# Ten wide idle products at the head of a retention and MLP kernel become 42 narrow ones

## The chip, the cores and the metric

The kernel runs on one core of a Trainium2 chip. A core has a matrix engine (TensorE, PE in the profile; its weight loads are listed apart as PEld), three engines for elementwise work (VectorE = DVE, ScalarE = ACT, GpSimd = POOL), a fifth that only issues transfers (SyncE = SP), and 16 DMA engines. Each engine works off its own stream of instructions in order, and the engines wait for each other by semaphores. The metric is the device time of one execution in microseconds (us); lower is better.

## The reference

Two stages follow each other. The first is a retention: attention without softmax, with a decay per head. For 8 batches, 8 heads, 576 positions and head dimension 64:

```python
scores = scale * np.matmul(q, k.transpose(0, 1, 3, 2))
Dmat = np.where(rel >= 0, gamma[:, None, None] ** rel, 0.0)   # rel = query position - key position
attn = np.matmul(scores * Dmat, v)
```

Its output, turned to 4608 tokens by 512 features, goes through a feed-forward layer with a "snake" activation and 2048 hidden features:

```python
h = x @ w_in
s = np.sin(alpha * h)
out = (h + s * s / (alpha + 1e-9)) @ w_out
```

All inputs and the output are in float32.

## The kernel before

The products are made in float16 and summed in float32. The decay is separable, so q and k are multiplied by powers of gamma when they are cast (`cast`, L126, by a table `cn`), and only a triangular mask is left for the scores. The 512 first positions of a batch are worked as two parts p of 256 positions, each in two chunks of 128; what earlier chunks contribute comes through a running state of 64 x 64 per head. The 64 last positions of all batches are worked at the end (`Ends`).

For one batch, the steps on TensorE are: `turn` (L189) transposes q and k by products with an identity; `scores` (L325) makes k times q in quadrants of 64 x 64; `outer` (L262) makes the sums of k times v for the state; `values` (L353) multiplies the masked scores with v, once for `same` False and once for True, and TensorE drains between the two (`change_rows`, L214); `add_states` (L385) adds what the state contributes. `masked` (L342, VectorE) applies the mask, `take_sum`, `more`, `next_sum` and `to_state` make the states (ScalarE, GpSimd, VectorE), and `keep` (L403) casts the result to xT, the input of the second stage. In this stage a product is small: 64 or 128 columns, so many instructions pass in a short time.

The second stage works on 512 tokens at a time (n = 0 to 8). `project(n, fc)` (L501) makes 128 of the 2048 hidden features with four products of 512 columns; `sine` (ScalarE), `square` (one of three engines) and `product` (VectorE) make the activation gT; `gemm2(n, u)` (L547) adds four products of 512 columns to an output tile, and `finish` writes it. The weights are loaded once, by GpSimd's queue, in four groups each: `load_w_in(g)` (L91) and `load_w_out(g)` (L95), 512 KB a group in float16.

The order of everything is written out by hand. Under `tc.manual_schedule()` (L582) the order of the calls is the order of each engine's stream. The first blocks are interleaved call by call (L583 to L1067): attention of batch 0, then `project` of block 0 mixed with attention of batch 1, and so on. From block 3 on a loop (L1072) places the attention of batch n + 1, mostly at unit 12 of the 16 units of block n, between the second stage's steps.

At the head TensorE has nothing to do until q and k have arrived and been cast. There `keep_busy` (L562) puts idle products on it: products of a tile of zeros with itself, whose result nobody reads. Each product has its own weight load ahead of it, so one idle product is two instructions. A call takes a PSUM tile under a tag, and the first product of a call waits for the last product of the call before it with the same tag. There are four calls ahead of the first `turn` (L593 to L596), of 2, 8, 10 and 4 products of 512 columns; the first waits for the tile of zeros (L591) alone. Two further calls, of 4 products and 1, stand among the steps of batch 0 (L616, L636).

Behind the head, in TensorE's order: `turn` of q and k, part 0; `turn` of k, part 1; scores(0, 1); idle products; `turn` of q, part 1; outer, scores, outer and two more scores; one idle product; values(0, False); a small transpose of alpha; values(0, True); add_states(0); values(1, False), values(1, True), add_states(1); project(0, 0) in two halves, for which the first group of w_in must be there; and project(0, 6) (L664), the first product that needs the second group.

The lines that the change touches, and the function:

Of the kernel before, what the change touches and what calls it, by code (L numbers as in the profile page):

```python
# [17 lines left out]
def kernel(  # L18
# [543 lines left out]
    def keep_busy(n, tag, m=512):  # L562
        idle = psum.tile([P, 512], F32, tag=tag, bufs=1, name="idle")
        for _ in range(n):
            matmul(idle[:, 0:m], zero[:, 0:P], zero[:, 0:m], start=True, stop=True)
# [16 lines left out]
    with tc.manual_schedule():  # L582
# [9 lines left out]

        keep_busy(2, "h0")  # L593
        keep_busy(8, "op")
        keep_busy(10, "op")
        keep_busy(4, "op")  # L596
        load(0, "q", 0)
        cast(0, "q", 0, G_, (1,))
# [601 lines left out]
```

## Time and profile before

| | us |
|---|---|
| median of 3 runs (lowest, highest) | 313.68 (312.84, 314.13) |
| the profiled execution | 313.16 |
| its span, first to last instruction | 311.4 |
| TensorE busy | 298.4 (96% of the span) |
| VectorE, ScalarE, GpSimd busy | 207.3, 183.3, 140.4 |
| mean clock granted to TensorE | 0.993 |
| moved by DMA | 49.96 MB, mean 160 GB/s |

The profile is of one execution. Its lines name an engine, a source line (L565 is line 565 of the kernel; a helper's line stands for all its calls), an operation, the tiles it writes and reads, and a count. What stands in brackets is how long the engine was idle before it, and what ended that idle time; "issue" means that the engine waited for nothing that the profile shows. Times of the timeline count from the start of the span. Matmuls overlap in the pipeline, so their modelled durations are longer than the distance from one start to the next. "PEclk" is the share of full clock that TensorE was granted. The queues q8 and q14 carry instructions, q0 the transfers that GpSimd issues (the weights), q1 those of SyncE.

### The profile page before, as it was taken

The page shows a single profiled execution, that of the slowest core. Times are in us where ns is not written, and L with a number is a line of the kernel's source. Part 1 is how long each engine was busy: PE and PEld are TensorE (multiplying, and loading weights), DVE is VectorE, ACT ScalarE, POOL GpSimd, SP SyncE. Part 2 cuts the span into 40 slices and gives each one's busy share as a digit, 9 for nine tenths or more (in the row PEclk, how much of TensorE's full clock was granted, in tenths as well). Part 3 has the DMA queues.
Part 4 walks back from the last instruction along what each step waited for, and adds up shares of the span by engine and source line. Part 5 has one row for each costly group of instructions (what it writes and reads, how often), then busy time and mean ns, then how long its engine had stood idle before and what let it go on. Part 6 is the DMA issues. An engine that isn't in the chain of part 4 may idle for free.

```text
span 311.4 us, 7830 instructions
## 1 busy us (share of the span) xinstructions
PE 298.4 (96%) x3238; PEld 150.7 (48%) x3238; DVE 207.3 (67%) x283; ACT 183.3 (59%) x292; POOL 140.4 (45%) x151
## 2 busy tenths in 40 slices
PE   8779989999999999999999999999999999999994
PEld 2455645445554544454445444544454454444443
DVE  2578998689778798576766676656666746655500
ACT  1328942678457767775677567756664456555411
POOL 2855665973919657989275927560030000000000
PEclk9989999999999999999999999999999999999999
DMA  8999999999797579979797979773532111111232
GB/s 208 289 231 258 218 252 269 238 229 235 197 244 208 103 117 310 227 117 218 196 272 118 237 187 281 97 144 76 117 66 44 34 36 36 34 35 34 51 86 67
DMA packets 103107, 49.96 MB, mean 160 GB/s; under 512 B 44944, under 2 KB 98592, under 8 KB 103072
## 3 DMA queue, kind: packets, MB, share of 16 engines
q1 hardware_dynamic: 98192, 44.99, 64.2%
q0 software_dynamic: 4224, 4.19, 8.0%
q8 instruction: 25, 0.41, 0.6%
q10 hardware_dynamic: 656, 0.28, 0.4%
q14 instruction: 10, 0.08, 0.1%
HBM read 36.85 MB, written 9.44 MB: 149 GB/s over the span
## 4 chain that ended last, share of the span: by engine, by line
PE 82%; DMA 6%; DVE 4%; ACT 3%; issue 2%; SPq 1%; POOL 1%; ACTq 0%; DVEq 0%
PE ops L552 38%; PE hps L509 36%; DMA w_in<-in_moe_w_in_dram 3%; PE o L374 3%; PE sc L334 2%; DMA v<-in_v_dram 2%; DVE gT L533 2%; ACT s_t L517 2%; PE kv L275 1%; SPq L114 1%; DVE ss_t L528 1%; DVE q L162 1%; PE o L396 1%; ACT ss_t L526 1%; POOL ss_t L528 0%
## 5 line engine op out<-in xcount | busy, mean ns | idle before, releaser
L552 PE MATMUL ops<-w_out,gT 128*128 128x512 f16 (+1 forms) x592 | 143.5, 374 | 1.2 <-DMA w_out<-in_moe_w_out_dram 1.1
L517 ACT ACTIVATE s_t<-hps,alpha_t 128x512 f16<-128x512 f32 x144 | 97.9, 685 | 74.8 <-PE hps L509 74.0
L533 DVE SCALAR_TENSOR_TENSOR gT<-ss_t,inva,hps 128x512 f16<-128x512 f16 x144 | 106.0, 745 | 50.1 <-ACT ss_t L526 46.0
L509 PE MATMUL hps<-xT,w_in 128*128 128x512 f16 (+1 forms) x568 | 128.2, 360 | 2.0 <-DVE gT L533 1.8
L509 PEld LDWEIGHTS <-w_in 128*128 128x128 f16 x632 | 61.4, 98 | 66.1 <-issue 3.2
L552 PEld LDWEIGHTS <-gT 128*128 128x128 f16 x592 | 56.2, 98 | 64.1 <-issue 2.0
L528 DVE TENSOR_TENSOR ss_t<-s_t 128x512 f16<-128x512 f16 x67 | 40.7, 607 | 21.6 <-ACT s_t L517 21.1
L526 ACT ACTIVATE ss_t<-s_t 128x512 f16<-128x512 f16 x69 | 43.3, 630 | 1.6 <-DVE gT L533 0.5
L345 DVE TENSOR_TENSOR ret<-sc,mask 128x1024 f16<-128x1024 f32 x32 | 38.7, 1218 | 4.0 <-PE sc L334 3.9
L162 POOL TENSOR_TENSOR k<-k,cn 128x1024 f16<-128x1024 f32 (+1 forms) x17 | 29.2, 1723 | 22.4 <-DMA k<-in_k_dram 22.4
L103 ACT COPY osb<-ops 128x512 f32<-128x512 f32 (+1 forms) x34 | 19.5, 573 | 18.1 <-PE ops L552 16.5
L162 POOL TENSOR_TENSOR q<-q,cn 128x512 f16<-128x512 f32 (+1 forms) x16 | 24.4, 1537 | 7.5 <-DMA q<-in_q_dram 6.1
L317 POOL TENSOR_TENSOR kvs<-s,kvs 128x256 f32<-128x256 f32 x23 | 17.2, 747 | 5.3 <-ACT kvs L103 3.8
L103 ACT CAST xT<-o 128x1024 f16<-128x1024 f32 (+1 forms) x14 | 13.4, 957 | 9.0 <-PE o L396 8.9
L146 POOL TENSOR_TENSOR ks<-ks,cn 128x512 f16<-128x512 f32 x4 | 4.2, 1043 | 29.3 <-PE o L374 29.3
L509 PE MATMUL hps<-xS,w_in 128*128 128x512 f16 x64 | 16.4, 379 | 0.0
L316 POOL TENSOR_TENSOR s<-kvs,cn 128x256 f32<-128x256 f32 x23 | 14.1, 613 | 3.6 <-ACT kvs L103 3.3
L528 POOL TENSOR_TENSOR ss_t<-s_t 128x512 f16<-128x512 f16 x8 | 9.3, 1163 | 14.3 <-ACT s_t L517 11.5
L105 POOL CAST v<-v 128x1024 f16<-128x1024 f32 (+1 forms) x15 | 15.0, 1002 | 0.9 <-DMA v<-in_v_dram 0.8
L309 POOL TENSOR_TENSOR s<-kvs,cn 128x256 f16<-128x256 f32 x19 | 12.1, 638 | 7.3 <-DVE kvs L105 5.4
L103 ACT COPY kvs<-kv 128x256 f32<-128x256 f32 (+2 forms) x15 | 7.9, 548 | 10.1 <-PE kv L275 8.4
L374 PE MATMUL o<-ret,v 64*64 64x128 f16 x512 | 12.3, 222 | 1.3 <-DVE ret L345 0.7
(53 smaller groups left out, 135.2 us busy)
## 6 DMA issues: line engine op xcount, KB each, us to landing
out_dram<-osb SPq DMA_DIRECT2D x70, 128.0 KB, 3.1
q<-in_q_dram SPq DMA_DIRECT2D x16, 512.0 KB, 7.1
k<-in_k_dram SPq DMA_DIRECT2D x16, 512.0 KB, 5.9
v<-in_v_dram SPq DMA_DIRECT2D x16, 512.0 KB, 6.6
w_in<-in_moe_w_in_dram POOLq DMA_DIRECT2D x4, 512.0 KB, 9.3
w_out<-in_moe_w_out_dram POOLq DMA_DIRECT2D x4, 512.0 KB, 9.9
ks<-in_k_dram SPq DMA_DIRECT2D x8, 128.0 KB, 4.8
qs<-in_q_dram SPq DMA_DIRECT2D x8, 128.0 KB, 3.9
```

What stands on the lines that cost most here:

```text
L103: eng.copy(d_, s_)
L105: eng.tensor_copy(d_, s_)
L162: eng.tensor_tensor(dst[:, a0:a1].rearrange("p a r t d -> p t (a r) d"), t_.rearrange("p (t a) x -> p t a x", t=2)[:, :, a0:a1].rearrange( ...
L317: nc.gpsimd.tensor_tensor(self.kvs[:, c], s32, self.kvs[:, c], ADD)
L345: nc.vector.tensor_tensor(ret.rearrange("p t (z x) -> p (t z) x", z=2), sc.rearrange("p t (z x) -> p (t z) x", z=2), mask[:, 0:256].unsque ...
L374: made.append(matmul(o[t][halves(e), c : c + 128], v16[halves(g), 4 * t + 2 * x + e, r, :], self.ret[p, x][halves(g), t, m : m + 128], sta ...
L509: matmul(hps_of[n, fc][0][:, cols], w_in16[:, a, fc * P : (fc + 1) * P], xs[n][:, a, cols], start=(a == 0 and part != 1), stop=(a == KT - ...
L517: nc.scalar.activation(s_t, hps, mybir.ActivationFunctionType.Sin, bias=0.0, scale=alpha_t[:, fc : fc + 1],)
L526: nc.scalar.activation(ss_t, s_t, mybir.ActivationFunctionType.Square)
L528: eng.tensor_tensor(ss_t, s_t, s_t, MULT)
L533: nc.vector.scalar_tensor_tensor(gT[n][:, fc, :], ss_t, inva[:, fc : fc + 1], hps, MULT, ADD)
L552: matmul(ops[n, c, cols.start][:, cols], gT[n][:, fk, c * P : (c + 1) * P], w_out16[:, fk, cols], start=(fk == 0), stop=(fk == FC - 1), sk ...
```

## The change

The third call at the head makes 42 products of 128 columns where it made 10 of 512:

```diff
         keep_busy(2, "h0")
         keep_busy(8, "op")
-        keep_busy(10, "op")
+        keep_busy(42, "op", 128)
         keep_busy(4, "op")
         load(0, "q", 0)
         cast(0, "q", 0, G_, (1,))
```

`keep_busy` has had the third parameter m, the number of columns, all along. The columns that stream through TensorE in this call go from 5120 to 5376. The products of a call have no waits among each other, and the tile, the tag and the wait at the first product stay as they are. With a weight load for each product, TensorE's stream has 64 more instructions from there on. No other engine's stream changes.

## The prediction

> **What bounds the kernel now.** I read the page first: which engine is full, and who feeds it with instructions.
>
> ```profile
> span 311.4 us, 7830 instructions
> PE 298.4 (96%) x3238; PEld 150.7 (48%) x3238; DVE 207.3 (67%) x283; ACT 183.3 (59%) x292; POOL 140.4 (45%) x151
> PEclk9989999999999999999999999999999999999999
> q8 instruction: 25, 0.41, 0.6%
> ```
>
> TensorE is busy for 96% of the span, so a pause in it costs its whole length, except in the first stretch, where the weights arrive. Queue 8 brings instructions: 0.41 MB in 25 packets is 16 KB each, and TensorE's 6476 records over 25 packets make about 256 instructions a packet; no other engine has so many.
>
> Then the timeline of TensorE, first 30 us:
>
> ```profile
> 1.23 8.48 PE L565 MATMUL idle<-zero 128*128 128x512 f16 x24 [1.23 <-DVE zero L591]
> 9.54 0.61 PE L195 MATMUL tr<-ident,q 128*128 128x128 f16 x8
> 9.99 0.61 PE L195 MATMUL tr<-ident,k 128*128 128x128 f16 x8
> 11.05 0.62 PE L195 MATMUL tr<-ident,k 128*128 128x128 f16 x8 [0.45 <-POOL k L162]
> ...
> 20.07 0.31 PE L396 MATMUL o<-qT,s 64*64 64x128 f16 x8 [1.39 <-issue]
> ...
> 21.69 1.89 PE L509 MATMUL hps<-xT,w_in 128*128 128x256 f16 x8
> 23.75 6.55 PE L509 MATMUL hps<-xT,w_in 128*128 128x512 f16 x35 [0.17 <-DMA w_in<-in_moe_w_in_dram]
> ```
>
> At 18.69 TensorE stops for 1.39 us and waits for nothing that the profile shows. The view of busy time by stretches explains it, and shows the clock beside it (columns: stretch, length, then busy time and count of PE, PEld, DVE, ACT, POOL, then granted clock, DMA share, GB/s):
>
> ```profile
> 0.00:18.69 18.69, 14.97 (x222) 7.84 (x223) 9.01 (x13) 4.53 (x7) 11.82 (x16) 1.00 1.03 243
> 20.05:51.95 31.90, 30.30 (x383) 17.31 (x383) 28.24 (x39) 19.66 (x33) 17.09 (x20) 0.95 1.19 246
> ...
> 13.76:17.17 3.41, 2.17 (x113) 1.67 (x113) 2.69 (x3) 1.02 (x3) 3.27 (x5) 1.00 1.20 250
> 17.17:20.59 3.42, 1.51 (x57) 1.05 (x56) 2.76 (x7) 0.16 (x1) 3.06 (x5) 1.00 1.19 216
> 20.59:24.00 3.41, 3.15 (x44) 2.01 (x42) 1.89 (x3) 1.82 (x4) 0.00 (x0) 0.50 1.17 276
> 24.00:27.41 3.41, 3.41 (x17) 1.56 (x16) 2.83 (x6) 2.47 (x5) 2.54 (x3) 1.00 1.20 219
> ```
>
> From 20.05 to 51.95 there are 383 products, 383 loads and two drains: 768 = 3 x 256. At 51.80 the products' start times show a second pause, 0.27 us to 52.07, again with no wait in the instruction behind it. So both pauses lie on the ends of 256-instruction blocks. The DMA view, narrowed, has queue 8's packets starting at 17.84 and 49.76: TensorE went on 2.23 and 2.31 us after those starts. That is an instruction fetch arriving late.
>
> Last, the chain that ended last and the waits: the chain goes through the transfer of w_in's second group (13.70 to 23.70), and at 41.84 TensorE waits 1.06 us for a w_out group:
>
> ```profile
> 13.70 10.00 DMA w_in<-in_moe_w_in_dram
> 23.70 0.05 issue
> 23.75 8.62 PE hps L509 x44
> ...
> 41.84 1.02 PE L552 MATMUL ops<-w_out,gT 128*128 128x512 f16 x4 [1.06 <-DMA w_out<-in_moe_w_out_dram]
> ```
>
> The eight weight transfers run end to end on the software queue from 15.1 to 50.7 us and no head product releases them; so TensorE gains nothing by being early at 23.75 and may be about 1 us late before 41.84.
>
> **The change, part by part.** *The products themselves.* Ten products of 512 columns go, 42 of 128 come. The ten start at 5.73; the starts are 427 ns apart until 6.93 and 215 after it. A 128-column product with its load costs 56 ns at full clock (the eight turns of q, 9.542 to 9.933). At the slow clock no row shows one: the ends are 56 and 427 ns. I take 107, a quarter of 427, because columns set the price in the nearest row (256 columns at clock 0.50 in the line at 21.69: 213 ns). So 11 run slow until 6.93 and 31 at 56 ns; the last starts at 8.60, ends 0.22 later, and with the 0.06 us of the hand-over seen at 8.68 the last four begin at 8.88 instead: 0.2 us late. By the ends it is 0.4 early (all at 56) or 0.7 late (427 each until 6.93). The turns of q and k and VectorE's row of takes, casts and masks behind them (dense from 10.64 to 19.93) move by 0.2; k's second turn waits for POOL anyway. Cover: the wait at 23.75. If that cover were gone it would cost 0.2.
>
> *The first late block.* The end of each block moves 64 places up. The one at 18.69 now falls into values(0, False), at today's 17.62. Its fetch is asked for earlier too. I fitted the place: packets start most evenly when counted from 45 instructions before the end of the block before the last fetched; from there to the packet's start takes 3 to 7 us while the transfers are dense (first 60 us), 1.6 to 4.3 up to 125 us, and 1.2 to 2.4 after 130 us. For the first packet that place was passed at 13.27 and is now passed at 11.06 (the turn of k). With the same 4.57 and 2.23 us the block is there at 17.9; values(0, False) needs it at 17.8. The stall of 1.39 becomes about 0.1 (0 to 2.4, by delays of 3 to 7). TensorE gains 1.3 us, and ACT's keep and the project(0, 0) behind it start at 20.6 instead of 21.69. The gain ends at 23.75: there w_in's second group is late next. Worth to the end: 0.
>
> *The clock.* The clock is granted anew every 3.41 us: 17.17, 20.59 and 24.00 above. A stretch with 2.17 us of busy kept it, one with 1.51 lost half of it for the next 3.41. Today the lost one (20.59 to 24.00) is hidden: project(0, 0) ends just as the weights land. After the change values, add_states and both halves of project(0, 0) are done by about 22, and 20.59 to 24.00 holds 1.2 us of busy at full clock (0.43 + 0.43 + 0.25 and a remainder), less than the 1.51. So 24.00 to 27.41 runs at half clock, where TensorE has no pause: 1.7 us late. At 41.84 up to 1.06 of that is absorbed; but POOL's squares follow these products and issue the w_out groups, so not all: 0.65 to 1.7, and 1.0 taken. Without the idle window: 0.
>
> [...]
>
> *The block at 51.80.* Its fetch is asked for 0.6 us earlier (44.77 to 44.19), and needed 0.8 earlier (51.07): 44.19 + 4.98 + 2.25 = 51.42, a stall of 0.35 for 0.27 now. Plus 0.1 (-0.3 to +1).
>
> *The block at 138.* This is new. Today a block ends at 144.98, amid slow steady 512-column products, and its fetch has 5.7 us to spare. Moved up 64 places, the end comes at 138.07, and its request just before the attention's small products, at 134.88. Between them the stream runs dense:
>
> ```profile
> 52.06:134.88 82.82, 80.71 (x963) 41.64 (x966) 65.44 (x81) 55.96 (x88) 59.63 (x61) 1.00 0.93 209
> 134.88:138.07 3.19, 3.19 (x158) 2.40 (x159) 2.36 (x3) 2.62 (x5) 2.58 (x4) 1.00 1.01 126
> ```
>
> Over 300 instructions in 3.19 us, and the fetch needs 1.73 (its delay today, 135.30 to 137.03) + 2.27 = 4.0: a stall of 0.8 us (0.2 to 1.5 by 1.2 to 2.4). Nothing covers it: after 110 us TensorE has no pause of 0.25 us or more in which it could be made good. All other blocks keep 3.6 us or more.
>
> [...]
>
> *Sum.* 0 + 0 + 1.0 + 0.1 + 0.8 = +1.9 us on the profiled execution's 313.16 (span 311.4 and 1.8 around it), 315.06. The median of the runs, 313.68, lies 0.52 higher; on it the sum is 315.58. I take the middle, 315.3.
>
> **The rivals.** *The fetch at 138 is late, the clock stays* (the windows fall so that the idle time at 22 is split between two): +0.9, 314.1 to 314.6. For it: where the windows begin is not the kernel's to choose. Against: about 1.8 us of idle in windows of 3.41.
>
> *Nothing shows:* fetches at 138 at the short end, the head hidden: 313.2 to 313.9. For it: 23 of 25 blocks arrive in time today.
>
> *Faster:* the stall at 18.69 is on the path after all. This needs w_in's second group to land by 22.3 instead of 23.70, so that 1.39 comes through, and 0.27 at 51.80 vanishes: 313.16 - 1.66 = 311.5 (to 312.1). Against: the software queue is continuous from 15.1.
>
> *The narrow products don't wake the clock* at 6.93 but a window later, 10.35: 42 x 107 + 4 x 427 ns from 5.73 end at 12.1, the turns come 2.6 us late, 1.06 of it absorbed at most: +1.5 to 2.6, with the block at 138 316.0 to 317.5. Against: TensorE is as busy with them.
>
> **How the numbers follow.** Forecast 0.50 (its own range 314.2 to 316.8), clock stays 0.20, nothing shows 0.12, faster 0.10, not woken 0.08. A measurement of this kernel tells about 0.5%, 1.6 us, from no change, so slower starts at 315.25. Of the forecast's half, 0.43 lies above; with the last rival slower is 0.51. Same is 0.07 + 0.20 + 0.12 = 0.39, faster 0.10. The range 313.0 to 316.9 leaves out the faster case and the ends.
>
> **What would show it.** Right: the four wide idle products begin near 8.9; no pause of 1 us near 18.7, but an idle stretch before 23.75; clock 0.50 in a window after 24; a pause without a releaser near 138 to 139 of 0.2 to 1.5 us, packets of queue 8 about 2.2 us ahead of it. Wrong: w_in landing earlier or later than 23.7; the pause at 18.69 unchanged (then blocks are not what I counted); no pause near 138.

## The result, and the profile after

The changed kernel took 314.89 us (median of 20 executions, 313.16 to 317.54), the kernel before 313.24 (20 beside them, 312.47 to 315.03). The ratio is 1.0056, 95% interval 1.0039 to 1.0074: about 1.65 us slower. The times of the changed kernel fall into two groups, one around 313.8 and one around 316, which the experiments below explain. The profiled execution of the changed kernel belongs to the shorter ones, 313.45 us with a span of 311.7, against 313.16 and 311.4 before. So it shows only a part of the loss.

Of the page, the lines that answer to those of before:

```profile
span 311.7 us, 7894 instructions
...
PE 296.9 (95%) x3270; PEld 151.8 (49%) x3270; DVE 206.6 (66%) x283; ACT 183.0 (59%) x292; POOL 140.4 (45%) x151
...
PEclk9979999999999999999999999999999999999999
...
q8 instruction: 25, 0.41, 0.6%
```

There are 64 instructions more, and all on TensorE (32 products, 32 loads). The other engines have their old counts.

TensorE's timeline, first 30 us:

```profile
1.23 7.65 PE L565 MATMUL idle<-zero 128*128 128x512 f16 x56 [1.23 <-DVE zero L591]
8.71 0.61 PE L195 MATMUL tr<-ident,q 128*128 128x128 f16 x8
...
17.70 0.74 PE L374 MATMUL o<-ret,v 64*64 64x128 f16 x16 [0.67 <-DVE ret L345]
...
21.10 1.34 PE L509 MATMUL hps<-xT,w_in 128*128 128x256 f16 x8
24.16 6.02 PE L509 MATMUL hps<-xT,w_in 128*128 128x512 f16 x33 [1.72 <-DMA w_in<-in_moe_w_in_dram]
```

The stop of 1.39 us without a releaser, at 18.69 before, is gone. The two halves of project(0, 0) start at 21.10 and not at 21.69. What was gained is then spent on the next line: TensorE waits 1.72 us for w_in's second group, and goes on at 24.16, where before it waited 0.17 and went on at 23.75.

At 51.80 there was a pause of 0.27 us inside the three values. It made the row of their 48 products 1.41 us long in the kernel before; now the row takes 1.15. Before, then after:

```profile
50.92 1.41 PE L374 MATMUL o<-ret,v 64*64 64x128 f16 x48
```

```profile
50.90 1.15 PE L374 MATMUL o<-ret,v 64*64 64x128 f16 x48
```

And near 138 there is a pause that the kernel before does not have. Before, then after:

```profile
136.44 0.41 PE L396 MATMUL o<-qT,s 64*64 64x128 f16 x16
136.78 1.04 PE L509 MATMUL hps<-xT,w_in 128*128 128x512 f16 x4
137.65 1.89 PE L552 MATMUL ops<-w_out,gT 128*128 128x512 f16 x8
```

```profile
135.77 0.41 PE L396 MATMUL o<-qT,s 64*64 64x128 f16 x16
136.11 1.04 PE L509 MATMUL hps<-xT,w_in 128*128 128x512 f16 x4
136.99 0.81 PE L552 MATMUL ops<-w_out,gT 128*128 128x512 f16 x3
138.57 1.25 PE L552 MATMUL ops<-w_out,gT 128*128 128x512 f16 x5 [0.77 <-issue]
```

An instruction packet starts on queue 8 at 136.00, 2.57 us before TensorE goes on. Counted from the ends at 18.69 and 51.80, which moved up 64 places, the product at 138.57 is the first of its block of 256.

The first line of these two views is a useful marker, since TensorE's waits show nothing behind it but this pause (0.77 us here, none in the kernel before). From its start to the end of the span it is 174.94 us in the kernel before and 175.92 here: the stretch with the pause is 0.97 us longer. Up to the marker this execution was 0.67 quicker than the one before (135.77 against 136.44).

### The profile page after: what moved, and what is told of

Its sections match the earlier page's. It is cut to its first block, busy times and chain, and to the rows that moved or that the text cites. A ratio compares the mean times of both kernels' runs of the same rounds, so it can differ in the third digit from the quotient of the medians.

```text
span 311.7 us, 7894 instructions
## 1 busy us (share of the span) xinstructions
PE 296.9 (95%) x3270; PEld 151.8 (49%) x3270; DVE 206.6 (66%) x283; ACT 183.0 (59%) x292; POOL 140.4 (45%) x151
## 4 chain that ended last, share of the span: by engine, by line
PE 81%; DMA 10%; DVE 2%; ACT 2%; issue 2%; POOL 1%; ACTq 0%; DVEq 0%
PE ops L552 38%; PE hps L509 35%; DMA w_in<-in_moe_w_in_dram 3%; DMA w_out<-in_moe_w_out_dram 3%; PE sc L334 3%; DMA v<-in_v_dram 2%; PE o L374 2%; DMA q<-in_q_dram 1%; PE kv L275 1%; ACT s_t L517 1%; PE o L396 1%; POOL k L162 1%; DVE ss_t L528 1%; DVE gT L533 0%; DVE s L309 0%
## 5 line engine op out<-in xcount | busy, mean ns | idle before, releaser
L528 DVE TENSOR_TENSOR ss_t<-s_t 128x512 f16<-128x512 f16 x67 | 39.8, 593 | 23.0 <-ACT s_t L517 22.5
L309 POOL TENSOR_TENSOR s<-kvs,cn 128x256 f16<-128x256 f32 x19 | 12.0, 633 | 5.2 <-DVE kvs L105 3.2
```

The costliest lines, as they stand in the source:

```text
L528: eng.tensor_tensor(ss_t, s_t, s_t, MULT)
```

## The experiments

Unless said otherwise, times are medians with their range, beside the kernel before on the same chip: 313.25 us (29 executions) in the first group of runs, 313.29 (23) in the second. "The tail" is the time from the marker just shown to the end of the span.

**The changed kernel again**, as the measure for the rest of its group.

> The changed kernel once more beside the three above. Theory: ratio 1.003 to 1.008; its executions fall in two groups, at 313.2 to 315.0 with a mean granted clock of 0.994 or more, and at 315.6 to 317.5 with 0.981 to 0.989; the pause of 0.6 to 0.9 us at 138 stands in either. If the clock's windows cost it, an execution of the slower group shows clock 0.50 in a stretch behind 23.7 us.

Measured: 315.35 us (313.55 to 316.65, 12 executions), ratio 1.0059 (1.0038 to 1.0080). In its trace the pause before 138.91 is 0.77 us and the tail 175.89.

**The same count, other widths.** Eight wide products stay, and 34 of 32 columns follow, which makes 42 again with few columns:

```diff
-    def keep_busy(n, tag, m=512):
+    def keep_busy(n, tag, m=512, more=0):
...
-        for _ in range(n):
+        for m in n * [m] + more * [32]:
...
-        keep_busy(42, "op", 128)
+        keep_busy(8, "op", 512, 34)
```

> The ten idle products stay wide in eight, and 34 products of 32 columns stand behind them: 42 products as in the change, 5184 columns. If the count of instructions is what matters, and not the width of 128: pause at 138 us of 0.6 to 0.9 us, none of over 1 us at 18.7, median 1 to 2 us over before as in the changed kernel. If the narrow products matter by their width (the clock, their own price): time differs from the changed kernel's by over 0.3%.

Measured: 315.21 us (313.88 to 317.06, 6), ratio 1.0074 (1.0049 to 1.0099); a pause of 0.54 before 138.97, tail 175.71. As far as six executions can tell, it is the number of instructions that matters here, and not the width of the products.

**Sixteen instructions more** than the change, 80 in all:

```diff
-        keep_busy(42, "op", 128)
+        keep_busy(50, "op", 104)
```

> 50 idle products of 104 columns instead of 42 of 128: 80 instructions more than before, 16 more than the change. The block end near 138 us moves 16 places further up, to 136 to 136.6 us, deep in the dense stage. Theory: its fetch is asked for at the same time, so the pause grows from 0.8 to about 2.2 us (1.5 to 2.8), and the median lies 1 to 2 us over the changed kernel's. Rival: cost by the instruction: the 16 more change nothing that shows.

Measured: 316.60 us (315.70 to 317.86, 4), ratio 1.0114 (1.0087 to 1.0141). In TensorE's timeline the pause now stands ahead of the last product of the marker's row, and is three times as long:

```profile
136.66 0.40 PE L396 MATMUL o<-qT,s 64*64 64x128 f16 x15
139.43 0.24 PE L396 MATMUL o<-qT,s 64*64 64x128 f16 x1 [2.37 <-issue]
```

The sixteen instructions moved the end of the block from among the 512-column products, whose starts are 216 ns apart there, up to the end of the small ones, 16 of which pass in 0.34 us (both in the profiled execution of the change). Counted from the marker, TensorE needs the block at 0.40 us where it was 2.03, and gets it at 2.77 where it was 2.80: the need came 1.6 us earlier, and the fetch did not. The tail is 177.59, 2.65 longer than before. The first block was late here too, by 1.36 us ahead of 18.03, but project(0, 6) starts at 24.28, between the 24.16 and 24.55 of the changed kernel.

**A whole block.** The change stays, and 24 projections of blocks 1 and 2 are made in two halves (256 columns a product), 8 instructions more for each. That is 192 more, 256 with the change's 64, and all of them stand ahead of the place near 138: from there on the blocks end where they ended before. Against the changed kernel:

```diff
-        project(1, 2, "m1")
+        project(1, 2, "m1", 0)
+        project(1, 2, "m1", 1)
...
```

> The changed kernel, and 24 projections of blocks 1 and 2 in two halves: 192 instructions more between 57 and 130 us, so that with the 64 of the change the stream has moved by 256, one whole block, and its ends beyond 130 us stand where they stood in before. Theory of the block ends: no pause at 138 us; what stays is the head's part (idle before 24 us, clock at half in some executions), so a median of 0.3 to 2 us over before with a wide spread, 0.7 under the changed kernel. Rival (more instructions cost by themselves): 256 more cost more than 64, over 1.0056.

Measured: 314.99 us (312.93 to 317.22, 12), ratio 1.0050 (1.0022 to 1.0079). In its trace the pause is gone:

```profile
136.20 0.41 PE L396 MATMUL o<-qT,s 64*64 64x128 f16 x16
136.54 1.04 PE L509 MATMUL hps<-xT,w_in 128*128 128x512 f16 x4
137.41 1.89 PE L552 MATMUL ops<-w_out,gT 128*128 128x512 f16 x8
```

The tail is 175.0, that of the kernel before, and this execution took 312.96. Yet the spread is as wide as the changed kernel's, and the median only 0.36 lower, where 0.7 was expected; a spread of 4 us does not tell the two apart. So there is a second cause, ahead of 57 us, since the kernel is up to there the changed one.

**The late block without the head.** The kernel before, with eight projections of block 1 in halves: 64 instructions more, but only from 57 us on: project(1, 2), (1, 5), (1, 7), (1, 1), (1, 3), (1, 0), (1, 6) and (1, 11). Against the kernel before:

```diff
-        project(1, 2, "m1")
+        project(1, 2, "m1", 0)
+        project(1, 2, "m1", 1)
...
```

> The head is the one of before; 64 instructions are added between 57 and 100 us instead, by making eight projections of block 1 in two halves (the same columns, eight more loads and products each). Theory of the block ends: the end that stands at 145 us moves up to the attention stage and TensorE pauses 0.6 to 0.9 us near 138 us, with the pause of 1.39 us near 18.7 us unchanged; the halves cost under 0.1 us. Time 0.7 us over before (ratio 1.002), and no executions of 315 us and more, as the head and its clock are untouched. Rival (it is the head alone that costs: idle stretch and clock): no pause at 138, time as before (ratio 1.000). Rival (64 more instructions cost by themselves, anywhere): as the changed kernel, ratio 1.0056.

Measured: 313.39 us (312.96 to 315.03, 12), ratio 1.0012 (0.9993 to 1.0031). In the one execution that was traced the pause is there, and the tail is 176.20, 1.26 longer:

```profile
140.02 1.25 PE L552 MATMUL ops<-w_out,gT 128*128 128x512 f16 x5 [1.11 <-issue]
```

The pause is longer than the 0.6 to 0.9 expected; the packet itself took 1.60 us, and 1.10 in the profiled execution of the change. But the median rose by 0.14 only. The interval, -0.2 to 1.0 us, holds the 0.7 that was expected and also no loss at all, so this run alone does not show the block's cost in the time. Nor does its trace show a typical execution: it is one of the three longest, at 314.87 us, with the clock at half from 19.39 to 26.22. Between 65 and 80 us it is 0.62 us quicker than the first trace of the kernel before, because a wait of TensorE on VectorE at 70 us is gone; the section on what was not expected comes back to it. Whether that offsets the pause in the other executions was not seen.

**Four idle products in the gap.** The change's 64 instructions, with four of the idle products moved behind project(0, 0), where TensorE waits for w_in:

```diff
-        keep_busy(42, "op", 128)
+        keep_busy(38, "op", 136)
...
         project(0, 0, "m1", 1)
+        keep_busy(4, "h1")
```

> The changed kernel with four wide idle products put between project(0, 0) and project(0, 6), into the idle stretch ahead of w_in's second group; 38 narrow products of 136 columns instead of 42 of 128 make up for their eight instructions, so the block ends beyond 24 us are the changed kernel's. If the idle stretch ahead of 24 us costs the clock of the busy stretch behind it, most executions of 315 us and more go: median 313.5 to 314.0, what is left being the pause at 138. If the spread has another cause, the median stays at 314.9 to 315.4.

Measured: 313.67 us (313.43 to 314.32, 12), ratio 1.0016 (1.0003 to 1.0029). The changed kernel's spread of 3 to 4 us has become 0.9. The pause at 138 stays, 0.41 us, with a tail of 175.55.

**Both mended.** The same four products in the gap, and 112 instructions in place of 64, so that the blocks end at other places:

```diff
-        keep_busy(42, "op", 128)
+        keep_busy(62, "op", 84)
...
         project(0, 0, "m1", 1)
+        keep_busy(4, "h1")
```

> 62 idle products of 84 columns, and four wide ones ahead of project(0, 6): 112 instructions more than before. By the places of the blocks and the delays of the packets in the trace of before, no block is late: none at 18.7, none at 52, none at 138. With the clock kept as in the kernel that fills the idle stretch, the median is 0 to 1 us under before (312.3 to 313.3). If the idle stretch is not filled well, executions of 315 us and more remain.

Measured: 313.01 us (312.52 to 314.41, 12), ratio 0.9995 (0.9981 to 1.0009). There is no late block at 18.7, at 52 or at 138, and the tail is 174.95. It is the best of the variants, and not to be told from the kernel before. Beside the kernel with the four products alone it shows what the block at 138 costs where the clock is kept (mean 0.998 in its profiled execution, 0.997 in that kernel's): the medians are 0.66 apart and the tails 0.60, and eleven of the twelve times here lie under all twelve there.

**The block moved by idle products alone.** The three calls of 8, 10 and 4 become one of 150 narrow ones, 256 instructions more than before:

```diff
-        keep_busy(8, "op")
-        keep_busy(42, "op", 128)
-        keep_busy(4, "op")
+        keep_busy(150, "op", 64)
```

> 150 idle products of 64 columns stand in place of the 22 wide ones of the second, third and fourth call: 256 instructions more, all narrow, so every block end beyond the head stands at the instruction where it stood in before. Theory of the block ends: the pause of about 1.4 us at 18.7 is there as in before, none at 138; time as before, ratio 0.998 to 1.003. If narrow idle products or more instructions cost by themselves: over 1.006, as there are four times as many as in the change.

Measured: 314.68 us (313.87 to 316.07, 6), ratio 1.0056 (1.0034 to 1.0078). The expectation of no loss was wrong, but not for the block at 138: there is no pause, and the tail is 174.97 us. Where 1.4 us near 18.7 was expected, TensorE waits 1.79 us ahead of 21.75; the profile puts the end of that down to a state of GpSimd (`s`, L309), and a packet of queue 8 had started 2.52 us earlier. The loss comes from the head. The narrow products were over too early, at 7.3 us, and the view by stretches (length, busy time and count of PE, PEld, DVE, ACT, POOL, then granted clock, DMA share, GB/s) shows 0.98 us of work in a window behind them, and the next window at clock 0.50:

```profile
7.75:11.17 3.42, 0.98 (x15) 0.64 (x13) 1.05 (x3) 1.01 (x1) 3.18 (x3) 1.00 1.16 293
11.17:14.58 3.41, 3.40 (x28) 1.73 (x29) 2.36 (x2) 1.01 (x1) 1.35 (x2) 0.50 1.17 264
```

project(0, 6) starts at 25.11 there, 1.36 us later than before. The marker comes 0.69 later.

**Three single executions of the changed kernel**, each traced, to see one of each group.

> The changed kernel again, for a trace of one of its slower executions, of which the two traces of it so far had none (about half of its timed executions are such). If this one has 315 us or more: theory, a stretch at clock 0.50 begins between 23.4 and 26 us behind a stretch with an idle time of 1.4 to 2.7 us ahead of w_in's second group, TensorE's place at 41 us is then 0.6 to 1.7 us behind that of the faster executions, and the pause at 138 is the same 0.8 to 1.1. Rival: the clock is full behind 24 us and the time is lost elsewhere.

> As the first look at the changed kernel: with 315 us or more, clock 0.50 in a stretch that begins between 23.4 and 26 us; with less, full clock there.

> As the first look at the changed kernel: with 315 us or more, clock 0.50 in a stretch that begins between 23.4 and 26 us; with less, full clock there.

Measured: 315.82, 315.56 and 313.63 us. In the second, the view by stretches:

```profile
20.61:24.03 3.42, 0.92 (x8) 0.58 (x6) 2.99 (x7) 0.90 (x3) 0.00 (x0) 1.00 1.17 275
24.03:27.44 3.41, 3.20 (x8) 1.19 (x9) 0.52 (x2) 0.69 (x1) 2.54 (x3) 0.50 1.19 220
```

And in the third, over the same times:

```profile
20.61:24.03 3.42, 1.00 (x8) 0.65 (x8) 2.71 (x7) 0.69 (x1) 0.00 (x0) 1.00 1.17 275
24.03:27.44 3.41, 3.23 (x15) 1.49 (x16) 1.46 (x4) 1.81 (x3) 2.54 (x3) 1.00 1.19 219
```

The same work, the same gap ahead of it; from 24.03 on 8 products pass in the one and 15 in the other. In the second execution a clock window began at 20.61 and held 0.92 us of work, and the next, from 24.03, was granted 0.50. In the third the windows lay elsewhere (one of them from 22.32 to 25.73), and from 5.25 us to the end none was granted less than 1.00. In the first, three windows ran at half clock, from 17.88 to 28.12 (mean clock of the execution 0.984). The gap ahead of w_in does not explain all of that: the first of the three follows a window (14.47 to 17.88) with 1.95 us of batch 0's small products, and only the last, from 24.71, follows the gap. The two long executions reach the marker at 138.45 and 138.12, and the short ones (this third one, the profiled one and that of the repeat) at 136.24, 135.77 and 136.12. The tails are 175.59 to 175.92 in all five, and the pauses of the three are 0.46 to 0.50 where 0.8 to 1.1 was expected.

What the half clock costs further on is not read off the clock alone. TensorE's timeline in the second:

```profile
42.62 1.02 PE L552 MATMUL ops<-w_out,gT 128*128 128x512 f16 x4 [0.36 <-DMA w_out<-in_moe_w_out_dram]
44.05 0.61 PE L195 MATMUL tr<-ident,q 128*128 128x128 f16 x8 [0.40 <-DVE kT L105]
```

and in the third:

```profile
42.47 1.02 PE L552 MATMUL ops<-w_out,gT 128*128 128x512 f16 x4 [0.52 <-DMA w_out<-in_moe_w_out_dram]
43.33 0.61 PE L195 MATMUL tr<-ident,q 128*128 128x128 f16 x8
```

Behind the wait for w_out only 0.15 us of delay is left. But VectorE was as late as TensorE had been: it starts its cast of q at 41.11 in the second and at 39.69 in the third, and between 32 and 43 us it is idle for 0.41 only, in both. TensorE waits for it, is 0.72 late at once, and 1.39 at 59 us. It is still 1.39 late at 67.83 (66.44 in the third). Then a wait on VectorE follows that the third does not have:

```profile
67.83 1.03 PE L509 MATMUL hps<-xT,w_in 128*128 128x256 f16 x8 [0.69 <-DVE gT L533]
72.37 1.90 PE L509 MATMUL hps<-xT,w_in 128*128 128x512 f16 x12 [0.56 <-DVE gT L533]
```

With it the second reaches the marker 1.88 behind the third. In the first execution it is the same: 1.79 late ahead of this wait, which is 0.47 long there, and 2.21 at the marker. So about 0.4 to 0.5 us of what the two long executions lose is this wait and not the clock; the section on what was not expected says where it comes from.

**The kernel before once more**, for a second trace of it.

> The kernel before, unchanged, for a second trace of it. In the traces of the changed kernel and its variants VectorE's square near 68.7 us takes 0.42 to 0.59 us in eight and 1.02 to 1.16 us in five, together with a wait of TensorE of 0.45 to 0.58 us at 70 to 72 us; in the one trace of the kernel before it takes 1.15 us, with a wait of 0.57. First theory: whether it is long depends only on whether a cast of q on GpSimd is running when the square starts, and so on when q and v land, in every kernel alike; then in this trace a square that starts inside a cast is long (1.0 us or more) and one that starts ahead of it is 0.42 us, and the wait at 70 us comes or goes with it. Rival: it belongs to the 64 instructions; then the square is long here whatever GpSimd does. In both cases the pauses of 1.4 us near 18.7 and 0.27 us near 51.8 are there, none near 138, and project(0, 6) starts at 23.7 to 23.9 if w_in's landing belongs to the kernel, at up to 24.5 if it varies by itself. Time 312.8 to 313.8.

Measured: 314.74 us, 313.73 in the execution beside it. This is one of the longer executions that the kernel before has too (5 of 52 in the two groups above lie at 314.3 or over). Its trace has the pauses at the places expected, both longer (1.68 us ahead of 20.34, 0.48 ahead of 54.68, none near 138), and a tail of 174.94; project(0, 6) starts at 23.98. VectorE's square starts inside a cast and takes 0.42 us, where the expectation had 1.0 or more for that; the section on what was not expected has the relation that fits in its place. The clock is half from 22.2 to 29.0: here the stop for the first block left 1.63 us of work in the window from 18.80 to 22.22, and the windows lay 1.6 us later than in the first trace, so that the lost one fell on w_in's products and not ahead of them. It held 2.72 us of work at half clock, and the next was at half clock too. TensorE reaches the marker at 137.99, 1.55 later than in the first trace. So the kernel before can have w_in's products at half clock too; of the changed one's first 20 executions nine are long (315.65 us or more), and the two long ones traced later both have it.

## Why the prediction was right

315.3 us was predicted, with 313.0 to 316.9 as the range; 314.89 was measured. The mechanisms were the right two, and the total came out nearly right; several terms inside it were mis-sized.

*The idle products.* Expected: the four wide ones 0.2 us later. In the second single execution, where the starts close up at the same point (6.96; before 6.93), the turn of q starts at 9.72 and before at 9.54: 0.18. Right, and hidden, as said. In the profiled one the starts of the wide products go from 427 to 215 ns apart at 4.65 us already, and the turn starts at 8.71; the wait for k takes that up (1.40 us there, 0.45 before). The 107 ns taken for a narrow product where the wide ones are 427 apart is what the second single execution shows: its starts are 106 to 107 ns apart until 6.96 and 56 after it, and the four wide ones begin at 8.86, where 8.88 was expected.

*The first late block.* Expected: 1.39 becomes about 0.1, worth 0 to the end. The packet starts at 15.27 in the profiled execution and TensorE shows a hitch of about 0.3 in values(0, False), 0.2 in two of the three single ones. Right. That TensorE's gain ends at w_in holds too. But project(0, 6) was 0.4 to 0.8 later than the 23.75 of before (24.16 to 24.55 in the five traces of the change; 23.98 in the second trace of the kernel before). A landing later than 23.7 was one of the text's signs of being wrong; it made the gap longer, and what holds the group up was not settled.

*The clock.* Expected: an idle stretch ahead of w_in, then a window at half clock from 24.0 to 27.4, worth 0.65 to 1.7, 1.0 taken. The window came at 24.03 to 27.44 in one execution, and with four idle products in the stretch the spread went from 3 to 4 us down to 0.9; the trace of that kernel has clock 1.00 from 17.5 to 27.7. That the gap costs time by the clock rests on these runs; but it is not a cost of 1.0 in each execution, and in the first single execution the clock was lost before the gap as well. Of the first 20, nine lie at 313.16 to 314.02, nine at 315.65 to 317.54, and two between. The text had "the clock stays" as a rival with 0.20, at 314.1 to 314.6; it is the other half of the same kernel, and quicker than that. And where the text let the wait at 41.84 absorb up to 1.06, that did happen (0.15 was left behind it), but the absorption did not last: VectorE, which has no such wait, brought the delay back. Ahead of the wait at 70 us the two long traces are 1.39 and 1.79 behind the third, where 0.65 to 1.7 was expected: the one with a single window at half clock is inside, the one with three just over. At the marker the long traces are 1.9 to 2.7 behind the short ones; the wait at 70 us, which the text did not have, is in that.

The mean granted clock doesn't sort the executions: the second of the three, at 0.995, is a long one, and the kernel with the idle products in the gap has one of 313.67 us at 0.988. A single whole window at half clock stands in the first trace of the kernel before (20.59 to 24.00, 313.16 us), in the profiled one of the change (18.30 to 21.72, 313.45 us) and in the second single one (24.03 to 27.44, 315.56 us), and three stand in the first (17.88 to 28.12, 315.82 us): where they fell told more here than how many there were.

*The block at 51.80.* Expected: +0.1 (-0.3 to +1). The pause is gone, so -0.27. The packet starts at 48.71 and the block is needed at 51.04, 2.33 later: just in time. A miss within its bounds.

*The block at 138.* Expected: a new stall of 0.8 (0.2 to 1.5). The pauses are 0.77, 0.77, 0.46, 0.50 and 0.47 us in the five traces of the change, and cost 0.64 to 0.97 in the tail. Right. With 256 or 112 instructions the pause goes; with 80 it is 2.37. "All other blocks keep 3.6 us or more" is right in that no other pause of this kind appears, but the room is less: in the third single execution a packet starts at 86.64 and its block is needed at 91.45, which leaves 2.5 us after the 2.3 from start to use.

*Where the fetch is asked for.* The text fitted a place, 45 instructions ahead of the end of the block before the last one fetched, and a delay from there to the packet of 1.2 to 2.4 us after 130 us. At the two late blocks this came out (4.1 us for the first and 1.77 for the one at 138 in the profiled execution, 4.57 and 1.73 taken). But for the other packets after 130 us of that execution the same place gives 0.4 to 5.2 us. So the place is a fit to one trace and not a rule; what the runs show is only that moving the block ends makes and removes the pause.

*The sum.* In a short execution only the tail loses, 0.6 to 1.0, less what is gained ahead of it. In the two long ones traced about 2 us come on top, 1.4 and 1.8 of it by the clock. The median of 20 lies between two groups of nine, so it is partly luck that it hits the predicted middle: that is the time of neither. In the same way the profiled execution gives the loss as 0.3, because it belongs to the shorter group and was 0.67 ahead at the marker.

## What to carry to other kernels

- TensorE's instructions came here in blocks of 256 (25 packets of 16 KB for 6476 records), and where a block was late TensorE stopped for 0.18 to 2.37 us. Adding or taking instructions far up moves every later end; look where the ends land. With 64 more an end came just behind the small products near 135 us, where the kernel before passes over 300 instructions in 3.19 us, and its packet started 2.57 us before TensorE went on. Padding by another count (112 in place of 64 here) moved the ends away again.
- TensorE came earlier here to a wait it could not shorten (1.72 us for w_in's second group in the profiled execution, 0.17 before), and the two long executions that were traced have a window at clock 0.50 behind that gap. With four idle products in the gap the trace has no such window there (1.00 from 17.5 to 27.7), and with the block at 138 out of the way as well no cost could be measured (ratio 0.9995). So look at what an engine does with time gained ahead of such a wait.
- When the times of a kernel fall into groups, one profile shows one group: trace some more before an average is explained.

## What the runs showed that was not expected

**How much work holds the clock.** In the first traces it looked like a matter of busy time alone: behind windows with 2.17 us of work (the kernel before) and 2.31 (its second trace) the next was granted 1.00, behind those with 0.92, 0.98, 1.51 and 1.63 it was granted 0.50. But in the profiled execution of the change these two lie the wrong way round:

```profile
14.89:18.30 3.41, 1.92 (x88) 1.36 (x81) 3.10 (x3) 0.52 (x2) 3.25 (x6) 1.00 1.21 223
18.30:21.72 3.42, 3.25 (x86) 2.49 (x78) 2.20 (x7) 1.52 (x3) 2.10 (x3) 0.50 1.19 216
21.72:25.13 3.41, 1.69 (x11) 0.89 (x10) 2.92 (x7) 0.83 (x3) 0.69 (x1) 1.00 1.17 279
25.13:28.54 3.41, 3.41 (x18) 1.52 (x16) 2.46 (x5) 2.92 (x5) 1.85 (x3) 1.00 1.17 250
```

1.92 us of mostly 64 x 64 products lost the clock for the next window, 1.69 of 128 x 128 ones kept it. Other traces agree: 1.95 us of small products (the first single execution, from 14.47) lost it, and 1.53 of large ones (the third, 22.32 to 25.73) kept it. So in these four windows the small products lost it with more busy time than the large ones kept it with. That is read from the traces, not tested by a run, and what decides it was not shown. Nor does busy time alone tell when the clock comes back: in the first single execution windows with 3.09 and 2.15 us at half clock were followed by another at half clock, and in the profiled one a window with 3.25 was not.

**A collision worth half a microsecond.** The wait of 0.57 us on VectorE at 70.67, which the first trace of the kernel before has and the profiled one after doesn't, goes with a cast of q on GpSimd. VectorE before, then GpSimd before:

```profile
68.62 1.15 DVE L528 TENSOR_TENSOR ss_t<-s_t 128x512 f16<-128x512 f16 x1
```

```profile
67.45 2.04 POOL L162 TENSOR_TENSOR q<-q,cn 128x512 f16<-128x512 f32 x2 [1.33 <-DVE gT L533]
```

and the same two after:

```profile
68.60 0.42 DVE L528 TENSOR_TENSOR ss_t<-s_t 128x512 f16<-128x512 f16 x1
```

```profile
68.79 2.13 POOL L162 TENSOR_TENSOR q<-q,cn 128x512 f16<-128x512 f32 x2 [1.87 <-DVE gT L533]
```

Before, the second cast runs from 68.45 to 69.49, and the square that starts at 68.62 ends 0.28 behind it. After, the square comes first and takes 0.42. In the 14 traces the square takes what is left of the cast plus about 0.28, and 0.42 at least: with 0.87 left 1.15 and 1.16, with 0.74 left 1.02, with 0.30 left 0.59, with 0.14 left (second trace of the kernel before) 0.42. The waits of 0.45 to 0.58 at 70 us come with the five squares of over 1 us and with no other. Two of these five are the two long executions of the changed kernel; none of its three short ones has the wait. Why the square lasts until the cast is over is not shown. The wait accounts for 0.57 of the 0.67 us by which the profiled execution was ahead at the marker, and most of the 0.62 that the kernel with the late block alone got back. The second trace of the kernel before is a long one and lacks the wait, and the first is a short one and has it; so it is not bound to the change, nor to being late alone. No run took the collision away by itself.

**Open.** Executions of the changed kernel above 317 us were never traced, so what they lose beyond the 2 us is not known. Nor is it known why w_in's second group landed later. That looks like a consequence of the changed head and not like chance: it lands at 23.70, 23.71 and 23.93 us in the three traces with the head of before, and at 24.11 to 24.60 in the eleven others.
